# mLSTM cell and multiplicative FFN on one core: one lasting PSUM tile for the cell, outputs first on VectorE, and unread products on TensorE

## The chip, the cores and the metric

The kernel runs on one core of a Trainium2 chip. The metric is the device time of one execution in microseconds (us), the median of several runs. A core has five engines that work side by side: TensorE (PE in the profile; its weight loads are shown apart as PEld), VectorE (DVE), ScalarE (ACT), GpSimd (POOL) and SyncE (SP), which here only issues transfers (DMA). They meet through semaphores.

## The reference, cut to what matters

Attention block: a recurrent cell over 768 time steps, for 4 batches and 8 heads of 40 dimensions. Then a feed-forward block on the 3072 x 320 result.

```python
for t in range(S):
    m_new = np.maximum(f_gate[:, :, t] + m, i_gate[:, :, t])
    f_stab = np.exp(f_gate[:, :, t] + m - m_new)
    i_stab = np.exp(i_gate[:, :, t] - m_new)
    C = f_stab * C + i_stab * np.einsum('bhd,bhe->bhde', vt, kt)
    n = f_stab * n + i_stab * kt
    h_tilde = np.einsum('bhde,bhe->bhd', C, qt)
    denom = np.maximum(np.abs(np.einsum('bhd,bhd->bh', n, qt)), 1.0)
    y[:, :, t] = sigmoid(o_gate[:, :, t]) * h_tilde / denom
...
a = x @ w1; b = x @ w2
out = ((a * b) @ w3) @ w_out        # 320 -> 1024 -> 1024 -> 320
```

All inputs of the cell are 32-bit floats. The weights come as 64-bit floats and are turned into 32-bit ones on the chip.

## The kernel before

The recurrence is computed in chunks. A unit n is one batch and 128 time steps (two chunks of 64), all 8 heads; there are 24 units, n = 0 to 23, four batches after each other for each stretch of time. Within a unit everything is a matrix product:

- ss = k times q, 64 x 64 for each head and chunk; VectorE multiplies it into the weights `pw` (L348), which ScalarE made with exponentials and GpSimd cut to a triangle;
- pc = what the unit adds to the state, from `kbuf` and the weighted values `vw` (`weighted`, GpSimd, L302). VectorE adds its first half to the state (`second`, L352, or copies it for the first four units, L354), GpSimd decays that (`decayed`, L307), and VectorE adds the second half (`after`, L362);
- ph = `pw` times the values and pi = q times the states before: the two parts of the output, taken one step later. VectorE adds them into `h` (L369, L373), makes the divisor `den` (three small operations, L378 to L381), multiplies it with the output gate (`o_in`, L383) and writes `y` (L385).

All four share one tile `cell` of four PSUM banks: ss and pc lie in banks 0 and 1 (columns 0 to 255 and 256 to 419 of 512), pi and ph in banks 2 and 3. It comes from a pool with one buffer and is allocated anew in every step (L314), so a step's first cell product waits until the last reader of the step before is done.

The main loop runs over steps s = 0 to 29. Step s does, among other things: transfers for later units (SyncE); `turn` of unit s, eight transposes of k and q on TensorE (`pt`, L93) with copies on ScalarE (L297); transposes of finished outputs (`px`, `x_trans`); the feed-forward products `pa`, `pb` (`up`, `up_rest`), from step 4 on; then `quarter_work`, with ph and pi of unit s - 1 and pc and ss of unit s on TensorE, and VectorE's work on them; then pieces of the conversion of the weights (`convert`, four VectorE operations each, L187 to L190). Later steps add the products `wp` that fold w3 and w_out into one matrix, and `po`, the last product. Ahead of the loop stand the gates: scans and subtractions on VectorE and GpSimd (L496 to L511), and products that turn and spread their results (`pg`, `ub`, `pd`).

TensorE works through its products in the order in which they are written (`in_order`). The other engines take their instructions in the order that a scheduler chose while the kernel was built, and from step 17 on in the written order; `tc.issue_after(x)` puts what it encloses behind instruction x. The order of the work on the cell before, on TensorE: ph, pi, pc, ss. On VectorE: `pw` (L348), the pc addition or copy (L352, L354), the outputs (L369 to L385), and last the second pc addition (L362).

A 32-bit product with plain operands shows as two records of TensorE in the profile, a transpose as one.

Of the kernel before, what the change touches and what calls it, by code (L numbers as in the profile page):

```python
# [8 lines left out]
FP = mybir.dt.float32  # L9
U32 = mybir.dt.uint32  # L10
AF = mybir.ActivationFunctionType
OP = mybir.AluOpType
# [4 lines left out]
def kernel(  # L17
# [26 lines left out]
    nc = tc.nc  # L44

    B, H, S, D = q.shape
    L = 64
    P = 128
    NT = S // L
    NT2 = S // P  # L50
    NU = NT2 * B
    NP = H // 2
    DP = 64
    D1 = D + 1
    DM = H * D
# [4 lines left out]
    REM = DM - KF * P  # L60
# [7 lines left out]
    sb = ctx.enter_context(tc.tile_pool(name="sb", bufs=2))  # L68
# [3 lines left out]
    ps_c = cell_psum.enter_context(tc.tile_pool(name="ps_c", bufs=1, space=bass.MemoryType.PSUM))  # L72
    banks = [ps_m]

    def mps(shape, name):
        pool = banks.pop(0)
        banks.append(pool)
        return pool.tile(shape, FP, name=name, tag="m")
# [3 lines left out]
    def in_order(ins):  # L82

        if last:
            tc.add_manual_dep(ins.ins, last.pop().name, mybir.DependencyInfo(
                mybir.DependencyClass.NoSync, mybir.DependencyReason.DATA), reason="in_order")
        last.append(ins.ins)

    def mm(out, lhsT, rhs, start=True, stop=True):
        in_order(nc.tensor.matmul(out, lhsT=lhsT, rhs=rhs, start=start, stop=stop))  # L90

    def transpose(out, in_, n=P):
        in_order(nc.tensor.transpose(out, in_, ident[0:n, 0:n]))  # L93

    halves = [slice(0, L), slice(L, P)]
    heads = [slice(0, D), slice(DP, DP + D)]
    quarters = ((0, 0), (1, 1), (0, 1), (1, 0))
# [8 lines left out]
    ident = const.tile([P, P], FP, name="ident")  # L106
# [10 lines left out]
    o_t, u_t = {}, {}  # L117
# [60 lines left out]
    def to_f32(dst, raw):  # L178
# [6 lines left out]
        r = wst.tile([128, n], U32, name="ma", tag="ma", bufs=1)  # L185
        V = nc.vector
        V.tensor_scalar(out=t, in0=hi, scalar1=3, scalar2=None, op0=OP.logical_shift_left)  # L187
# [70 lines left out]
    qT_t, kT_t, vw_t, before_t, y_t, x_t = {}, {}, {}, {}, {}, {}  # L258
# [51 lines left out]
    def quarter_work(s, rest):  # L310


        rest()
        t = ps_c.tile([P, 4, 512], FP, name="cell", tag="cell")  # L314

        def part(j, c0, n):
            return t[:, j:j + 2, c0:c0 + NP * n].rearrange("p x (n d) -> p x n d", d=n)

        ss, pc, pi = part(0, 0, L), part(0, NP * L, D1), part(2, 0, D1)
        ph = [t[halves[x], 2 + x, NP * D1:(NP + H) * D1].rearrange("p (h d) -> p h d", d=D1) for x in range(2)]  # L320
        n = s - 1
        if 0 <= n < NU:
            pw, vt, qT = u_t.pop(n), vbuf[n % NB], qT_t.pop(n)
            before = before_t.pop(n)
            for hd in range(H):
                for x, r in enumerate(halves):
                    mm(ph[x][:, hd, :], pw[r, hd, :], vt[r, hd, :])
            for p in range(NP):
                for hip, x in quarters:
                    mm(pi[halves[x], hip, p, :], qT[heads[hip], p, halves[x]], before[x][heads[hip], p, :])  # L330
        n, first_read = s, None
        if n < NU:
            c, b = divmod(n, B)
            kt, vw = kbuf[n % NB], vw_t.pop(n)
            ends = range(2 if c < NT2 - 1 else 1)
            first, second, after = state[b]
            before_t[n] = first, second
            state[b] = after, second, first
            for p in range(NP):
                for x, e in quarters:  # L340
                    if x in ends:
                        mm(pc[halves[e], x, p, :], kt[halves[x], 2 * p + e, :], vw[halves[x], 2 * p + e, :])
            kT, qT, pw = kT_t.pop(n), qT_t[n], u_t[n]
            for p in range(NP):
                for hip, x in quarters:
                    mm(ss[halves[x], hip, p, :], kT[heads[hip], p, halves[x]], qT[heads[hip], p, halves[x]])
            pv = pw.rearrange("p (n two) t -> p two n t", two=2)
            first_read = nc.vector.tensor_tensor(out=pv, in0=ss, in1=pv, op=OP.mult)  # L348
            with tc.issue_after(first_read.ins):

                if c:
                    nc.vector.tensor_tensor(out=second, in0=pc[:, 0], in1=second, op=OP.add)  # L352
                else:
                    nc.vector.tensor_copy(out=second, in_=pc[:, 0])  # L354
                if len(ends) > 1:
                    decayed(after, second, n, 1)
        done = None
        with tc.issue_after(first_read.ins) if first_read else nullcontext():
            if 0 <= s - 1 < NU:
                done = outputs(s - 1, pi, ph)  # L360
            if n < NU and len(ends) > 1:
                done = nc.vector.tensor_tensor(out=after, in0=pc[:, 1], in1=after, op=OP.add)  # L362
        return done

    def outputs(n, pi, ph):
        c, b = divmod(n, B)
        hs = slice(b * H, (b + 1) * H)
        h = sb.tile([P, H, D1], FP, name="h", tag="h")
        nc.vector.tensor_tensor(out=h.rearrange("p (n two) d -> p two n d", two=2), in0=pi,  # L369
                                in1=gT[:, c, hs].rearrange("p (n two) -> p two n", two=2).unsqueeze(3)  # L370
                                .to_broadcast([P, 2, NP, D1]), op=OP.mult)
        for x, r in enumerate(halves):
            nc.vector.tensor_tensor(out=h[r], in0=ph[x], in1=h[r], op=OP.add)  # L373

        den = sb.tile([P, H, 1], FP, name="den", tag="den")
        nc.vector.tensor_scalar(out=den.bitcast(U32), in0=h[:, :, D:D1].bitcast(U32), scalar1=0x7FFFFFFF, scalar2=None,  # L378
                                op0=OP.bitwise_and)
        nc.vector.tensor_scalar(out=den, in0=den, scalar1=1.0, scalar2=2.0, op0=OP.max, op1=OP.mult)  # L380
        nc.vector.reciprocal(out=den, in_=den)  # L381
        e = o_t.pop(n)
        nc.vector.scalar_tensor_tensor(out=e, in0=e, scalar=1.0, in1=den.to_broadcast([P, H, D]), op0=OP.add, op1=OP.mult)  # L383
        y_t[n] = sb.tile([P, DM + REM], FP, name="y", tag="y")
        return nc.vector.tensor_tensor(out=y_t[n][:, 0:DM].rearrange("p (h d) -> p h d", d=D), in0=h[:, :, 0:D], in1=e,  # L385
                                op=OP.mult)

    def send(n):

# [89 lines left out]
    def traced():  # L479
        return nc.cur_bb.bb.instructions  # L480
# [10 lines left out]

    f3, F3, U3, a3, w3d = (x.rearrange("p (c t) -> p c t", t=L) for x in (f_sb, F, U, a, w))
    V = nc.vector
    front = len(traced()) - 1

    V.tensor_copy(out=f_sb[third[0], 0:1], in_=a[third[0], 0:1])  # L496
# [4 lines left out]
    for i, r in enumerate(third):  # L501
        V.tensor_tensor_scan(out=M[r, 1:GC + 1], data0=F3[r, :, L - 1], data1=U3[r, :, L - 1], initial=M[r, 0:1],
                             op0=OP.add, op1=OP.max)
# [25 lines left out]
    for i, r in enumerate(third):  # L529
        nc.gpsimd.tensor_tensor(out=pick[r, :, i, :], in0=pair[r].to_broadcast([BH, B * NP, GC]), op=OP.mult,  # L530
                        in1=dec[r].unsqueeze(1).to_broadcast([BH, B * NP, GC]))
# [167 lines left out]
```

## Time and profile before

| what | value |
|---|---|
| median of 5 runs | 472.37 us (470.68 to 474.1) |
| the profiled execution | 469.81 us |
| its span on the core | 467.8 us |
| TensorE busy | 444.8 us, 95% of the span |
| VectorE busy | 257.8 us, 55% |
| ScalarE, GpSimd busy | 134.4 us, 82.2 us |
| moved by DMA | 52.72 MB, mean 113 GB/s |
| chain that ended last | PE 93%, issue 2%, all others 1% or less each |

A span is the time from the first to the last instruction of the profiled execution; the time of the run includes a little that lies around it (here 2.0 us). Busy times count the engine's records, which for TensorE overlap with its weight loads. The chain that ended last goes back from the last instruction, at each step to what released it. The slices cut the span into 40 equal parts of 11.7 us. The clock row gives what the throttle granted TensorE, in tenths of its full speed.

### The profile page before, as it was taken

To read this page: it belongs to the slowest core of one execution; us is meant where nothing else is said; L and a number is where in the kernel's file an instruction comes from. 1 tells how busy PE (TensorE), PEld (TensorE's weight loads), DVE (VectorE), ACT (ScalarE), POOL (GpSimd) and SP (SyncE) were. 2 spreads that over 40 slices of the span, in tenths; PEclk is the share of its full clock that TensorE was granted. 3 is DMA by queue.
4 is the path that set the end of the run, shared out by engine and by line. 5 is a ranking of instruction groups with operands and counts; after the bars stand their busy time and mean duration, and the time that the engine had idled before them with its cause. 6 is when DMAs were issued, how large, how long until landed. Compare 5 with 4: busy or idle time off the path is not lost.

```text
span 467.8 us, 12799 instructions
## 1 busy us (share of the span) xinstructions
PE 444.8 (95%) x5319; PEld 357.2 (76%) x5319; DVE 257.8 (55%) x515; ACT 134.4 (29%) x376; POOL 82.2 (18%) x156
## 2 busy tenths in 40 slices
PE   2866999999999999999999999999999999999997
PEld 2765788888778788887878777787777877868864
DVE  7675589888988988898832451615426134011110
ACT  3743274444443144223451230211101101011111
POOL 5341222222220222022161110200000000000000
PEclk9995699999999999999999999999999999999999
DMA  9999958688978677686452535444121120200001
GB/s 189 174 175 221 177 88 159 143 186 176 206 185 197 147 167 157 160 161 137 102 114 67 129 81 133 91 107 105 33 63 32 32 63 1 62 15 14 1 14 44
DMA packets 136554, 52.72 MB, mean 113 GB/s; under 512 B 109936, under 2 KB 127536, under 8 KB 136496
## 3 DMA queue, kind: packets, MB, share of 16 engines
q1 hardware_dynamic: 132896, 47.87, 50.0%
q10 hardware_dynamic: 3600, 4.03, 2.5%
q8 instruction: 42, 0.69, 0.7%
q14 instruction: 16, 0.13, 0.1%
HBM read 46.07 MB, written 5.80 MB: 111 GB/s over the span
## 4 chain that ended last, share of the span: by engine, by line
PE 93%; issue 2%; DVE 1%; POOL 1%; DMA 1%; ACT 1%; SPq 0%; POOLq 0%; DVEq 0%; ACTq 0%
PE pa L90 27%; PE po L90 23%; PE pb L90 18%; PE cell L90 13%; PE wp L90 7%; PE pt L93 2%; PE px L93 1%; DMA kbuf<-in_k_dram 1%; PE ub L90 1%; POOL pw L280 1%; POOL vw L302 0%; ACT pw L278 0%; SPq L444 0%; ACT qT L297 0%; PE pg L93 0%
## 5 line engine op out<-in xcount | busy, mean ns | idle before, releaser
L569 DVE TENSOR_TENSOR ab<-pb,a_sb 128x512 f32<-128x512 f32 x48 | 32.7, 689 | 139.5 <-ACT a_sb L568 139.5
L90 PE MATMUL po<-w3o,ab 128*128 128x320 f32 x384 | 106.2, 435 | 0.0
L90 PEld LDWEIGHTS po<-w3o,ab 128*128 128x128 f32 x384 | 72.1, 190 | 30.1 <-ACT a_sb L568 0.4
L90 PE MATMUL pa<-xT,w 128*128 128x256 f32 x384 | 92.8, 385 | 0.6 <-ACT xT L423 0.6
L90 PE MATMUL pb<-xT,w 128*128 128x256 f32 x384 | 90.7, 379 | 0.0
L90 PEld LDWEIGHTS pa<-xT,w 128*128 128x128 f32 x384 | 73.4, 193 | 13.5 <-ACT xT L423 1.0
L90 PEld LDWEIGHTS pb<-xT,w 128*128 128x128 f32 x384 | 73.0, 190 | 10.1
L568 ACT ACTIVATE a_sb<-pa 128x512 f32<-128x512 f32 x48 | 28.7, 598 | 169.0 <-PE pb L90 169.0
L307 POOL TENSOR_TENSOR state<-state,decay 128x164 f32<-128x164 f32 x40 | 22.0, 549 | 202.2 <-DVE state L352 133.2
L90 PE MATMUL pa<-xT,wr 64*64 64x256 f32 x384 | 47.0, 383 | 0.0
L90 PE MATMUL pb<-xT,wr 64*64 64x256 f32 x384 | 47.0, 383 | 0.0
L278 ACT ACTIVATE pw<-pw,aT 128x64 f32<-128x64 f32 x160 | 40.3, 337 | 14.3 <-DMA pw<-U_d 14.3
L90 PEld LDWEIGHTS pa<-xT,wr 64*64 64x64 f32 x384 | 25.8, 132 | 16.8 <-issue 7.8
L90 PE MATMUL wp<-wo,w3T 128*128 128x320 f32 x128 | 35.9, 433 | 0.6 <-DVE ab L569 0.6
L280 POOL TENSOR_SCALAR_AFFINE_SELECT pw<-pw 64x512 f32<-64x512 f32 x48 | 33.1, 690 | 18.6 <-ACT pw L278 17.0
L90 PEld LDWEIGHTS cell<-vbuf,pw 64*64 64x64 f32 x768 | 27.2, 140 | 8.6 <-issue 5.7
L348 DVE TENSOR_TENSOR pw<-cell,pw 128x512 f32<-128x512 f32 x24 | 16.6, 691 | 30.6 <-PE cell L90 30.6
L576 ACT COPY o_sb<-po 128x320 f32<-128x320 f32 x24 | 10.1, 422 | 75.4 <-PE po L90 75.4
L90 PE MATMUL cell<-vbuf,pw 64*64 64x41 f32 x768 | 27.2, 230 | 4.7 <-issue 4.7
L90 PEld LDWEIGHTS wp<-wo,w3T 128*128 128x128 f32 x128 | 23.7, 190 | 9.7 <-DVE ab L569 0.9
L90 PEld LDWEIGHTS pb<-xT,wr 64*64 64x64 f32 x384 | 25.8, 132 | 0.0
L373 DVE TENSOR_TENSOR h<-cell,h 64x328 f32<-64x328 f32 x48 | 23.9, 497 | 1.1
(90 smaller groups left out, 456.3 us busy)
## 6 DMA issues: line engine op xcount, KB each, us to landing
raw<-in_moe_w_dram SPq DMA_DIRECT2D x64, 128.0 KB, 3.1
pw<-U_d SPq DMA_DIRECT2D x40, 128.0 KB, 4.1
kbuf<-in_k_dram SPq DMA_DIRECT2D x24, 160.0 KB, 4.5
vbuf<-in_v_dram SPq DMA_DIRECT2D x24, 160.0 KB, 5.1
o_in<-in_o_gate_dram SPq DMA_DIRECT2D x24, 160.0 KB, 4.5
out_dram<-o_sb ACTq DMA_DIRECT2D x24, 160.0 KB, 2.0
raw<-in_moe_w_dram SPq DMA_DIRECT2D x7, 512.0 KB, 5.7
raw<-in_moe_w_out_dram SPq DMA_DIRECT2D x32, 80.0 KB, 3.0
```

The source lines that it names most:

```text
L90: in_order(nc.tensor.matmul(out, lhsT=lhsT, rhs=rhs, start=start, stop=stop))
L93: in_order(nc.tensor.transpose(out, in_, ident[0:n, 0:n]))
L278: nc.scalar.activation(out=pw[:, h, :], in_=src[:, h, :], func=AF.Exp, bias=aT[:, c, b * H + h:b * H + h + 1])
L280: nc.gpsimd.affine_select(out=pw[r], in_=pw[r], compare_op=OP.is_ge, fill=0.0, base=0, pattern=[[0, H], [1, L]], channel_multiplier=-1)
L307: nc.gpsimd.tensor_tensor(out=new, in0=old, op=OP.mult, in1=decay[:, b * NP:(b + 1) * NP, 2 * c + x:2 * c + x + 1] .to_broadcast([P, NP, D1]))
L348: first_read = nc.vector.tensor_tensor(out=pv, in0=ss, in1=pv, op=OP.mult)
L373: nc.vector.tensor_tensor(out=h[r], in0=ph[x], in1=h[r], op=OP.add)
L568: nc.scalar.mul(out=a_sb, in_=pa, mul=UP ** -2)
L569: nc.vector.tensor_tensor(out=ab_t[gr][j][:, fs[0]:fs[-1] + 1, t0:t0 + a_sb.shape[-1]], in0=pb, in1=a_sb, op=OP.mult)
L576: nc.scalar.copy(out=o_sb, in_=po)
```

## The change

The tile `cell` is allocated once, ahead of all loops, and used in every step. `keep_warm(times)` adds products of the identity with 92 of its own columns into columns 420 to 511 of bank 0 of `cell`, which nobody reads: 14 ahead of the gates' first instruction, and 3 in each of the steps 0 to 3, ahead of the step's cell products. On TensorE, ss now comes before pc. `outputs` is cut into three parts: h (its three operations) at once, then `first` (the divisor), then `then` (`o_in` and `y`). On VectorE the new order of a step is h, `pw`, the first pc addition or copy, the divisor, the second pc addition, `o_in`, `y`.

```diff
+    cell = ps_c.tile([P, 4, 512], FP, name="cell", tag="cell")
...
+    def keep_warm(times):
+        for _ in range(times):
+            mm(cell[:, 0, NP * (L + D1):512], ident, ident[:, 0:512 - NP * (L + D1)])
...
         rest()
-        t = ps_c.tile([P, 4, 512], FP, name="cell", tag="cell")
+        if s < B:
+            keep_warm(3)
+        t = cell
...
+            kT, qT, pw = kT_t.pop(n), qT_t[n], u_t[n]
+            for p in range(NP):
+                for hip, x in quarters:
+                    mm(ss[halves[x], hip, p, :], kT[heads[hip], p, halves[x]], qT[heads[hip], p, halves[x]])
             for p in range(NP):
                 for x, e in quarters:
                     if x in ends:
                         mm(pc[halves[e], x, p, :], kt[halves[x], 2 * p + e, :], vw[halves[x], 2 * p + e, :])
-            kT, qT, pw = kT_t.pop(n), qT_t[n], u_t[n]
-            for p in range(NP):
-                for hip, x in quarters:
-                    mm(ss[halves[x], hip, p, :], kT[heads[hip], p, halves[x]], qT[heads[hip], p, halves[x]])
+        den = None
+        if 0 <= s - 1 < NU:
+            den = outputs(s - 1, pi, ph)
+        if n < NU:
             pv = pw.rearrange("p (n two) t -> p two n t", two=2)
             first_read = nc.vector.tensor_tensor(out=pv, in0=ss, in1=pv, op=OP.mult)
...
-        done = None
-        with tc.issue_after(first_read.ins) if first_read else nullcontext():
-            if 0 <= s - 1 < NU:
-                done = outputs(s - 1, pi, ph)
+            if den:
+                done = den()
             if n < NU and len(ends) > 1:
-                done = nc.vector.tensor_tensor(out=after, in0=pc[:, 1], in1=after, op=OP.add)
-        return done
+                nc.vector.tensor_tensor(out=after, in0=pc[:, 1], in1=after, op=OP.add)
+            if den:
+                done = done()
+        return done if den else first_read
...
+    keep_warm(14)
     front = len(traced()) - 1
```

In the built program, the cell's first product of a step (in steps 1 to 3 now the first unread one) waits for the step before's second pc addition, and h waits for the last product of its step. The two reductions that make `pair` and `odd` (L474, L476), which stood at the head of VectorE's order, now stand behind the gates' last subtraction (L511). In SyncE's order, some of the later transfers of k (`load_turned`, from the tenth unit on) stand behind the transfers of a step's output instead of ahead of them. Nothing else moves.

## The prediction

> **What bounds the kernel now.** I read the page's slices first, then the busy time by stretch, then the chain of waits and the timeline of the one place where TensorE is not full. The slices (11.7 us each):
>
> ```profile
> PE   2866999999999999999999999999999999999997
> DVE  7675589888988988898832451615426134011110
> PEclk9995699999999999999999999999999999999999
> DMA  9999958688978677686452535444121120200001
> ```
>
> TensorE is full from the sixth slice on, at full clock. Only the first five hold anything to win, and two of those show a granted clock near half. Closer (us, then busy time and count for TensorE, its weight loads, VectorE, ScalarE, GpSimd; clock; DMA share; GB/s):
>
> ```profile
> 25.00:30.00 5.00, 3.73 (x120) 3.05 (x112) 2.95 (x7) 1.67 (x9) 1.55 (x3) 1.00 0.94 182
> 30.00:35.00 5.00, 2.35 (x111) 2.39 (x115) 4.70 (x10) 2.16 (x6) 2.67 (x4) 0.94 1.05 172
> 40.00:45.00 5.00, 3.04 (x86) 3.07 (x89) 3.84 (x10) 3.26 (x11) 0.24 (x1) 0.50 1.27 190
> 50.00:55.00 5.00, 4.43 (x13) 3.31 (x12) 4.68 (x12) 1.06 (x2) 2.57 (x5) 0.52 0.92 175
> 55.00:60.00 5.00, 5.00 (x145) 4.31 (x146) 1.13 (x2) 2.36 (x8) 0.00 (x0) 1.00 1.31 171
> 60.00:120.00 60.00, 58.91 (x1010) 50.48 (x1002) 53.74 (x118) 30.68 (x86) 16.89 (x30) 1.00 0.73 154
> ```
>
> From 60 us to the end TensorE is busy 403.5 of 407 us, so a step that arrives there earlier ends the kernel earlier by as much. Between 30 and 55 us it both waits and runs at half clock. What half clock costs, in the chain of waits (start, us, what):
>
> ```profile
> 48.14 1.91 PE pt L93 x8
> 51.24 3.75 PE pa L90 x8
> 69.27 1.02 PE pt L93 x8
> 70.29 1.73 PE pa L90 x8
> ```
>
> And why it waits, in the timeline around step 1 (start, us, engine, line, operation, idle before it):
>
> ```profile
> 27.55 0.69 DVE L348 TENSOR_TENSOR pw<-cell,pw 128x512 f32<-128x512 f32 x1 [1.97 <-PE cell L90]
> 28.40 0.49 DVE L369 TENSOR_TENSOR h<-cell,gT 128x328 f32<-128x328 f32 x1
> 30.61 0.72 DVE L383 SCALAR_TENSOR_TENSOR o_in<-o_in,den 128x320 f32<-128x320 f32 x1
> 31.36 0.82 DVE L385 TENSOR_TENSOR y<-h,o_in 128x320 f32<-128x320 f32 x1
> 32.22 0.33 DVE L362 TENSOR_TENSOR state<-cell,state 128x164 f32<-128x164 f32 x1
> 32.61 1.00 PEld L90 LDWEIGHTS cell<-vbuf,pw 64*64 64x64 f32 x31 [2.89 <-issue]
> ```
>
> TensorE ended step 1's cell products at 27.39; the next cell product starts when VectorE's last read of the cell banks (L362) ends at 32.55. The profile calls this "issue", but it is VectorE's chain of 5.2 us. After step 2 the same chain runs 37.36 to 41.86, 4.5 us, and is behind the gap up to 41.96.
>
> **What the Trainium skill says.** "TensorE: Matmul & The Clock Gate", Part 1: TensorE runs at half rate until it has been busy for a window of some 3.4 us, falls back after an idle window, and the windows run free of the kernel. The trace agrees on the factor two (above) and roughly on the length: the rates drop near 34.3 after 2.7 us of idleness and recover near 54.7, 3.5 us into products without a hole. It also shows a limit: 3.5 us of small products (ub, 17.8 to 21.4) stayed slow, so busy in the records is not surely busy for the gate. Before 24 us the clock column says 1.00, yet 32 ub products take 1.91 us at 8.78 and 1.08 us at 27.39: it was cold. The same page, Part 4, says transposes do not count as busy in the same way; no stretch here holds transposes alone. "PSUM — Partial Sum Buffer", PSUM bank collisions: engines must be kept apart by bank and quadrant, not by address. So unread products in an unused corner of bank 0 wait for bank 0's readers; in the built program they wait for the last reader of the whole tile.
>
> **The change part by part.** *VectorE's order.* The outputs' first three operations (h) now come first, e and y last; the pc1 addition, which frees the banks, stands before e and y. The built program makes h wait for the step's very last product, so nothing starts sooner; the banks are free sooner by e, y and gaps: 0.72 + 0.82 + 0.06 = 1.6 us after step 1, 0.49 + 0.49 + 0.07 = 1.05 after step 2. GpSimd's decay (0.46 us after pc0) is covered by three small operations, 0.17 + 0.17 + 0.20 us; if that fails, it costs 0.2. The chain is then some 3.5 us. y comes 0.3 us later relative to the banks; only step 5 has a px close behind it (a wait of 0.45 at 65.3), so 0.3 us there, elsewhere nothing: the other px take older tiles. pw comes 1.5 us later, read a step later.
>
> *ss before pc on TensorE.* pc waited for vw at 15.36 (1.55 us) and 26.23 (0.98). ss needs only qT, so up to 1 us of it moves into these waits.
>
> *One lasting tile.* No instruction; the waits between steps stay.
>
> *The pair and odd reductions* move behind the gate chain on VectorE (0.25 + 0.24 us at 8.42). pick started at 8.74 and still can; VectorE has 3.5 us free before 17.51. Nothing.
>
> *The unread products.* One f32 product is two records (weights 128 columns, 92 columns moving). No row has this shape. By the pt rows (128 columns of weights) a record is 1.91 / 8 = 0.24 us cold and 0.127 warm. Moving time alone, from pa, would be 92/256 of 0.47 = 0.17 cold, so weights bind; bounds 0.17 and 0.28, I take 0.24 and 0.12. Fourteen in front are 28 records, 6.7 us cold, from 1.6 us (identity ready at 1.54) to 8.3 at the latest, less if the clock rises meanwhile. The gates' first product came at 8.20: cost 0 to 0.2 us, cover TensorE's empty start. Three in each of steps 0 to 3 cost 1.4 us cold or 0.7 warm; as they wait for the banks they fill no bank wait, and in steps 2 and 3 stand on the path. In steps 0 and 1 they lie largely beside waits for qT and vw.
>
> **The sum.** Cold, the triple (1.4) eats what VectorE's order gives (1.6 and 1.05). The change pays by the clock. With the front products TensorE has no hole from 1.6 to 13.8 us, so I expect it warm at 7 to 12. Then ub(0) ends 0.8 earlier; the exps can start when ScalarE is free (10.07 instead of 10.80), and vw and pc follow by 0.7; step 0's cell ends near 15.8, not 17.34. In step 1 ScalarE's 16 exps, a scaling that needs a weight piece, and v(1) hold it: warm TensorE then idles about 2 us before qT and can lose the clock. Step 1 ends near 25.3 (2.1 early). Step 2: banks at 28.8; ub, pt and the triple leave no hole, so the clock is likely back while the cell products run: about 0.9 + 3.3 + the 1.2 us pause that stood inside this group at 35.58 (no wait in the profile, DMA full): 34.2, that is 3.2 early. Step 3: banks 3.5 later (37.7), triple and products 3.4 warm to 5.5 cold, 4.5 taken (a 2 us hole lies ahead), again a 1.2 us pause (46.06 before): 43.4, 4.7 early. Step 4 took 12.3 us from there to 60.45, of which the 3.75 pa would be 1.73 if warm; half of that and the pt gain: 11.6, ending at 55.0: 5.4 us early. From there TensorE is full. Profiled execution: span 467.8, with what lies around it 469.81; minus 5.4 is 464.4. That execution lies 2.6 us under the median of 472.37; against the median, **467.0**.
>
> **The rivals.** *The clock holds throughout.* Triple and products warm, 3.4 instead of 4.5 us in step 3 (42.3), step 4 in 9.7, with pt, px and pa at the rates of step 5: it ends at 52.0, 8.4 early: 464.0 against the median. For: the triples are there, and rates held at 65% busy windows (27.5 to 30.9). Against: a 2 us hole before each bank release, since the triple waits too.
>
> *Loads take the place.* DMA is over 0.9 busy in nearly every stretch to 60 us. k(3) was issued at 29.18 and takes 4.5 us, used at 37.3; k(6) at 54.38, used at 69.2. Those leave 3.6 and 10 us, so an advance beyond about 4 us can be clipped in steps 3 to 6; v(3), issued until 32.7, gates vw(3). Clipped to 1.5 us: 470.9.
>
> *Slower: triples on the path at half clock.* Place: steps 1 to 3, ahead of the first ph product. Price 1.4 each, 4.2, against 1.6 + 1.05 + 0.4; and if warm idling ahead of qT drops the clock at 24 instead of 34, step 2's ub, pt and ph run cold, 2.6 more: 3.8 later, less 1 us from ss: 475.2. It decides if less than one window in steps 2 and 3 is full.
>
> **How the numbers follow.** Forecast 0.47 (own range 464.5 to 469.8), clock held 0.24, loads 0.19, slower 0.10. About 0.5%, 2.4 us, is what a measurement of this kernel can tell from no change (its five runs spread over 3.4 us). Faster: 0.45 + 0.24 + 0.04 = 0.73; same 0.02 + 0.15 + 0.01 = 0.18; slower 0.09. The range, 461.8 to 471.6, takes in most of the held clock and of the loads; what is left out is mainly the slower case and the best of the held clock.
>
> **What would show it.** ub(0) in 1.1 us rather than 1.9 (front works); bank release 3.5 us after each cell group; clock column at 1.00 in part of 30 to 55; pa in step 4 at 1.7 or 3.75; step 4's cell end at 55. Wrong if TensorE's clock falls before 30 us and stays, if TensorE waits for kbuf or vbuf in steps 3 to 6, or if the total from step 5 to the end, 407 us, changes: then my claim that all lies in the first 60 us fails.

## The result and the profile after

| | before | after |
|---|---|---|
| median of the comparison | 470.72 us (79 runs) | 468.21 us (44 runs) |
| lowest, highest | 465.71, 474.76 us | 465.88, 470.92 us |
| ratio of the times | | 0.9963, 95% interval 0.9949 to 0.9976 |
| profiled execution, its span | 469.81, 467.8 us | 467.89, 466.1 us |

The change makes the kernel faster, by 2.5 us by the medians. Runs that lie over 1.5% above a kernel's fastest are left out of every ratio, and as the kernel before spreads over 9 us this leaves out more of its runs than of the others', so that a ratio shows less of a gain than the medians do (here 1.7 us). The kernel before was timed again with each group of experiments (its medians are 470.1 to 471.5 us). Below I give how far each kernel's median lies under that one, with the ratio and its interval behind it; differences under about 1 us between groups are not read.

The slices of the changed kernel, 11.65 us each:

```profile
PE   8697989999999999999999999999999999999997
DVE  6757898989988988898823350614416134011110
PEclk9977999999999999999999999999999999999999
DMA  8989997788995677597452625544021120200001
```

TensorE is at work from the first slice (the unread products in front), and two slices show the clock column at 7 in place of one at 5 and one at 6. The busy times by stretch of the changed kernel, with the columns as in the prediction:

```profile
25.00:30.00 5.00, 5.00 (x144) 4.92 (x142) 1.24 (x3) 0.84 (x2) 0.34 (x1) 0.50 0.85 163
30.00:35.00 5.00, 4.19 (x123) 3.79 (x124) 4.83 (x11) 3.65 (x12) 3.00 (x5) 0.98 0.94 183
40.00:45.00 5.00, 4.95 (x118) 4.78 (x120) 3.22 (x6) 1.15 (x2) 0.60 (x2) 0.54 0.93 132
50.00:55.00 5.00, 5.00 (x104) 4.23 (x107) 4.13 (x6) 1.72 (x6) 2.17 (x4) 1.00 0.91 133
60.00:120.00 60.00, 56.28 (x967) 47.86 (x966) 54.26 (x111) 28.28 (x79) 16.57 (x28) 1.00 0.81 167
```

Two places differ from the plan. From 25 to 30 us, where the kernel before ran at full clock, TensorE is busy without a hole but at half clock. And from 60 to 120 us it is busy 56.28 us, not 58.91: a loss in the part that I had called full. The transposes and the first feed-forward products of steps 4 and 5, in the chain of waits of the changed kernel:

```profile
45.76 1.78 PE pt L100 x8
48.63 1.99 PE pa L92 x8
...
66.36 1.02 PE pt L100 x8
67.38 1.73 PE pa L92 x8
```

pa of step 4 took 1.99 us, not 3.75: there the clock is up. The timeline around step 1's end, changed kernel:

```profile
28.72 0.50 DVE L383 TENSOR_TENSOR h<-cell,gT 128x328 f32<-128x328 f32 x1 [4.71 <-PE cell L92]
30.29 0.69 DVE L361 TENSOR_TENSOR pw<-cell,pw 128x512 f32<-128x512 f32 x1
31.94 0.28 DVE L374 TENSOR_TENSOR state<-cell,state 128x164 f32<-128x164 f32 x1
32.27 0.91 PE L92 MATMUL cell<-ident 128*128 128x92 f32 x6 [0.81 <-DVE state L374]
32.65 0.82 DVE L405 TENSOR_TENSOR y<-h,o_in 128x320 f32<-128x320 f32 x1
```

The cell products ended at 28.64 and the banks were free at 32.22: 3.6 us, where the old order took 5.2. The unread triple stands first behind the release. Step by step (end of the step's cell products, us):

| | step 0 | 1 | 2 | 3 | 4 | from there to the end |
|---|---|---|---|---|---|---|
| before | 17.35 | 27.39 | 37.36 | 48.14 | 60.39 | 407.4 |
| forecast | 15.8 | 25.3 | 34.2 | 43.4 | 55.0 | 407 |
| after | 16.28 | 28.64 | 35.64 | 45.76 | 56.01 | 410.1 |

So this execution was 4.4 us ahead when step 4 ended, against 5.4 in the forecast, and then lost 2.7 us. On the way, step 1 ended 1.25 us later than before. TensorE's waits in the changed kernel up to 64 us (us in total, times, longest) name two of the places:

```profile
PE cell L92 <- DVE state L374: 3.8, 2, 3.0
PE pt L100 <- DMA kbuf<-in_k_dram: 3.3, 1, 3.3
PE px L100 <- POOL y L435: 1.1, 1, 1.1
...
PE px L100 <- DVE y L405: 0.6, 1, 0.6
```

The prediction did not count k of unit 1 among the waits, and px waited 0.45 us before.

### The profile page after: what moved, and what is told of

It reads as the page before. It is cut to its first block, busy times and chain, and to the rows that moved or that the text cites. A ratio compares the mean times of both kernels' runs of the same rounds, so it can differ in the third digit from the quotient of the medians.

```text
span 466.1 us, 12891 instructions
## 1 busy us (share of the span) xinstructions
PE 448.5 (96%) x5371; PEld 362.5 (78%) x5371; DVE 262.2 (56%) x515; ACT 134.3 (29%) x376; POOL 82.6 (18%) x156
## 4 chain that ended last, share of the span: by engine, by line
PE 88%; DMA 4%; SPq 3%; DVE 2%; ACT 1%; issue 1%; POOL 1%; ACTq 0%
PE pa L92 27%; PE po L92 23%; PE pb L92 18%; PE cell L92 11%; PE wp L92 7%; DMA w3o<-in_moe_w_dram 2%; SPq L133 2%; PE pt L100 1%; PE px L100 1%; DMA kbuf<-in_k_dram 1%; DMA pw<-U_d 1%; SPq L178 1%; SPq L153 0%; ACT pw L285 0%; DVE ma L195 0%
## 5 line engine op out<-in xcount | busy, mean ns | idle before, releaser
L92 PE MATMUL pa<-xT,w 128*128 128x256 f32 x384 | 91.0, 380 | 0.8 <-ACT xT L445 0.8
L92 PEld LDWEIGHTS pa<-xT,w 128*128 128x128 f32 x384 | 72.3, 190 | 13.1 <-ACT xT L445 1.0
L314 POOL TENSOR_TENSOR state<-state,decay 128x164 f32<-128x164 f32 x40 | 19.2, 481 | 211.3 <-DVE den L395 159.2
L287 POOL TENSOR_SCALAR_AFFINE_SELECT pw<-pw 64x512 f32<-64x512 f32 x48 | 35.3, 735 | 13.3 <-ACT pw L285 11.8
L383 DVE TENSOR_TENSOR h<-cell,gT 128x328 f32<-128x328 f32 x24 | 12.0, 498 | 25.1 <-PE cell L92 25.1
```

The lines of the kernel that those rows point to most:

```text
L287: nc.gpsimd.affine_select(out=pw[r], in_=pw[r], compare_op=OP.is_ge, fill=0.0, base=0, pattern=[[0, H], [1, L]], channel_multiplier=-1)
L314: nc.gpsimd.tensor_tensor(out=new, in0=old, op=OP.mult, in1=decay[:, b * NP:(b + 1) * NP, 2 * c + x:2 * c + x + 1] .to_broadcast([P, NP, D1]))
```

## The experiments

Each edit is shown against the kernel that the text names.

**Orders or unread products.** Four kernels take the change apart; all are shown against the changed kernel. The first leaves out all unread products and keeps the two new orders and the lasting tile:

```diff
-        if s < B:
-            keep_warm(3)
...
-    keep_warm(14)
```

> The change without any unread product: new orders and the lasting tile alone. If the orders make the gain (banks released 1.6 and 1.05 us sooner after steps 1 and 2, ss ahead of pc), it is 1.5 to 3 us faster than before, ratio 0.994 to 0.997. If the clock makes it, the clock drops in step 1 or 2 and stays low until the first pa, as before, and the later px in step 5 (62.56 in the changed kernel) takes back what the banks gave: ratio 0.998 to 1.002.

Measured: 465.24 us, 6.0 less than before (ratio 0.9864, 0.9828 to 0.9901). It beats the changed kernel by 3 us.

The second keeps the unread products and the tile, with both old orders:

```diff
-            kT, qT, pw = kT_t.pop(n), qT_t[n], u_t[n]
-            for p in range(NP):
-                for hip, x in quarters:
-                    mm(ss[halves[x], hip, p, :], kT[heads[hip], p, halves[x]], qT[heads[hip], p, halves[x]])
             for p in range(NP):
                 for x, e in quarters:
                     if x in ends:
                         mm(pc[halves[e], x, p, :], kt[halves[x], 2 * p + e, :], vw[halves[x], 2 * p + e, :])
...
+            kT, qT, pw = kT_t.pop(n), qT_t[n], u_t[n]
+            for p in range(NP):
+                for hip, x in quarters:
+                    mm(ss[halves[x], hip, p, :], kT[heads[hip], p, halves[x]], qT[heads[hip], p, halves[x]])
...
+            if 0 <= s - 1 < NU:
+                done = outputs(s - 1, pi, ph)
             if n < NU and len(ends) > 1:
-                nc.vector.tensor_tensor(out=after, in0=pc[:, 1], in1=after, op=OP.add)
+                done = nc.vector.tensor_tensor(out=after, in0=pc[:, 1], in1=after, op=OP.add)
```

> The kernel before with the lasting tile and all unread products (14 in front, 3 in each of steps 0 to 3), orders on TensorE and VectorE as before. If the clock makes the gain: 2 to 4 us faster, ratio 0.991 to 0.996, as px in step 5 is not delayed. If the orders make it: the triples stand on the path, 0.7 to 1.4 us in each of steps 2 and 3, ratio 0.999 to 1.005.

Measured: 470.78 us, 0.5 less than before (0.9976, 0.9952 to 1.0000).

The third keeps only the 14 front products, the fourth only the triples, both with the new orders and the tile:

```diff
-        if s < B:
-            keep_warm(3)
```

> The changed kernel without the triples; the 14 products in front stay. If only the front lifts the clock (up at 13 us), step 0 is 1 us earlier but the wait for k of unit 1 (3.3 us before 21.9) drops it again, so this equals the version without unread products within 0.5 us. If the triples matter, the clock is not back at 30 and the time is 1 to 3 us above the changed kernel, ratio to before 0.998 to 1.003.

```diff
-    keep_warm(14)
```

> The changed kernel without the 14 products in front. If the front is worthless or harmful (it makes TensorE reach the wait for k of unit 1 early and lose the clock there), this is as fast as the changed kernel or up to 1.5 us faster: ratio to before 0.992 to 0.997, and the clock is high from about 24 us through step 1. If the front is what pays, 1 to 2 us slower than the changed kernel: 0.998 to 1.002.

Measured: front alone 465.47 us (5.8 less than before; 0.9866, 0.983 to 0.9902); triples alone 470.09 us (1.2 less; 1.0044, 1.0009 to 1.0079).

What follows: the front products neither win nor lose by themselves. The triples cost 5 us without them and 3 us with them. That the unread products pay is refuted: without any of them the kernel is faster.

**Which order.** Old VectorE order, ss ahead of pc on TensorE, lasting tile, no unread products. Shown is what differs from the kernel before with the lasting tile:

```diff
-            for p in range(NP):
-                for x, e in quarters:
-                    if x in ends:
-                        mm(pc[halves[e], x, p, :], kt[halves[x], 2 * p + e, :], vw[halves[x], 2 * p + e, :])
             kT, qT, pw = kT_t.pop(n), qT_t[n], u_t[n]
             for p in range(NP):
                 for hip, x in quarters:
                     mm(ss[halves[x], hip, p, :], kT[heads[hip], p, halves[x]], qT[heads[hip], p, halves[x]])
+            for p in range(NP):
+                for x, e in quarters:
+                    if x in ends:
+                        mm(pc[halves[e], x, p, :], kt[halves[x], 2 * p + e, :], vw[halves[x], 2 * p + e, :])
```

> The kernel before with the lasting tile and one more edit: on TensorE ss ahead of pc; VectorE's order as before, no unread products. Theory A (VectorE's order carries the gain of about 6 us that the two orders show together): the vw waits of steps 0 and 1 shrink by up to 1 us each, but the bank release stays 5.2 us after step 1's cell end, so the time is within 1.5 us of the kernel before (470.0 to 471.3). Theory B (ss first carries it: TensorE has no hole in front of pc, and VectorE's pw can start earlier): 466 to 467, and the cell ends of steps 1 and 2 come 1 us or more earlier than 27.39 and 37.36.

And VectorE's new order alone, same tile; against the kernel without unread products, it is the same move the other way round:

```diff
-            for p in range(NP):
-                for hip, x in quarters:
-                    mm(ss[halves[x], hip, p, :], kT[heads[hip], p, halves[x]], qT[heads[hip], p, halves[x]])
             for p in range(NP):
                 for x, e in quarters:
                     if x in ends:
                         mm(pc[halves[e], x, p, :], kt[halves[x], 2 * p + e, :], vw[halves[x], 2 * p + e, :])
+            for p in range(NP):
+                for hip, x in quarters:
+                    mm(ss[halves[x], hip, p, :], kT[heads[hip], p, halves[x]], qT[heads[hip], p, halves[x]])
```

> The kernel before with the lasting tile and VectorE's new order alone; TensorE keeps pc ahead of ss, no unread products. Theory A (VectorE's order carries the gain): bank release some 3.5 us after each cell end, time 465 to 467, within 1.5 us of the kernel with both orders (465.24). Theory B (ss first carries it): 469 to 470.5. Either way px of step 5 is late, by two waits of some 0.6 and 1.1 us, since GpSimd's decay follows the first pc addition.

Measured: 465.49 us (5.6 less; 0.9913, 0.9889 to 0.9936) and 466.08 us (5.0 less; 0.9901, 0.988 to 0.9923). Each alone brings nearly all that both bring together. Neither theory had that, and it pointed at what both kernels share: the tile.

Two more start from the kernel without unread products: GpSimd's copy of y at the head of the step, and six unread products in each of steps 2 and 3 that go to a rotating bank and so wait for nothing of the cell:

```diff
+        if 0 <= s - 2 < NY:
+            twice(s - 2)
...
-        elif 0 <= s - 2 < NY:
-            twice(s - 2)
```

> Both new orders and the lasting tile, no unread products, and one edit more: GpSimd's copy of y is issued at the head of its step, ahead of the weighting of v and the decay. Theory (VectorE's new order delays GpSimd's queue, and so step 5's px, by 1.6 us): the wait of 1.07 us on GpSimd ahead of px's later transposes goes, step 5's cell ends 1 us earlier than 64.33, and the time falls by about 1 us, from 465.24 to 464.2. Rival (TensorE meets another wait right behind, or loads take the place): 465 to 466.

```diff
+        warm = mps([P, 512 - NP * (L + D1)], "warm")
         for _ in range(times):
-            mm(cell[:, 0, NP * (L + D1):512], ident, ident[:, 0:512 - NP * (L + D1)])
+            mm(warm, ident, ident[:, 0:512 - NP * (L + D1)])
...
+        if 2 <= s < B:
+            keep_warm(6)
```

> Both new orders and the lasting tile, and 6 unread products in steps 2 and 3, written to a tile of the rotating four-bank pool, so that they wait for no bank of the cell and lie in the waits for the release (1.52 and 0.93 us without unread products). Theory path (unread products cost what stands behind the release): they cost at most 0.5 us in each step, time 464.5 to 466.5, against 468.21 of the changed kernel. Theory clock (filled waits keep the clock up): no drop of the granted clock between 30 and 50 us, 1 to 3 us faster than 465.24. Rival (any unread product costs, by its number): 12 products are 24 records of 0.12 us or more, 3 us or more slower than 465.24.

Measured: 465.47 us (5.6 less) and 467.67 us (3.4 less). The copy's wait of 1.07 us at px went, and the median did not follow. The filled waits cost 2.6 us: from step 1's end to the next cell product they added 0.55 us (4.17 against 3.62), after step 2 nothing (4.48 against 4.54). That is less than the loss. The profile shows part of the rest: this kernel is 1.1 us ahead of the one without unread products when step 4 ends (53.06 against 54.12), and then TensorE stops at 63.15 for 0.94 us inside step 5's products, without a wait. What such stops are is told next.

**The tile alone.** The kernel before, with the tile allocated once and nothing else:

```diff
+    cell = ps_c.tile([P, 4, 512], FP, name="cell", tag="cell")
...
-        t = ps_c.tile([P, 4, 512], FP, name="cell", tag="cell")
+        t = cell
```

> The kernel before with the lasting tile alone: both old orders, no unread products. It is the control for the kernels with one new order each, which both gained 5 us. Theory (the tile itself is worth nothing; each order alone already takes nearly all that there is to gain): within 1 us of the kernel before, 470 to 472. Rival (the gain that both orders share is the tile's, and the unread products took it back where old orders and unread products stood together): 465 to 467.

Measured: 466.81 us, 3.9 less than before (0.9935, 0.9912 to 0.9959). Its 22 runs lie between 463.39 and 468.55 us, the 63 of the kernel before between 465.54 and 475.13. The edit that I had put at nothing carries the larger part of the gain. The rival that the scheduler gave the other engines another order falls: in the two traces the instructions of VectorE, ScalarE, GpSimd and SyncE (518, 406, 165 and 424, without those for semaphores) stand in the same order. The built programs show how they differ: a tile allocated anew makes the first cell product of steps 2 and 3 wait for three semaphores (a transfer, VectorE, TensorE's own earlier work), the lasting tile for two. The Trainium skill ("Perfetto Trace Analysis", Identifying Dependency Chains) says that an instruction waiting on several engines may get semaphore instructions of their own in front of it. So it is in these traces: before, the instruction in front takes the transfer and VectorE, and TensorE's own semaphore stays on the product; with the tile kept, it takes the transfer alone and is over in 0.05 us, and VectorE's stays on the product. The chain of waits shows the two cases. First the kernel before (start, us, what):

```profile
29.98 2.66 issue
32.65 2.93 PE cell L90 x118
35.58 1.29 issue
...
41.96 4.10 PE cell L90 x108
46.06 1.17 issue
47.24 0.90 PE cell L90 x20
```

and the same stretch with the tile kept:

```profile
32.42 0.34 DVE state L364
32.76 0.04 issue
32.81 4.59 PE cell L92 x124
...
41.53 0.34 DVE state L364
41.87 0.04 issue
41.91 3.69 PE cell L92 x126
```

Before, the chain breaks off at "issue": the wait sits in a semaphore instruction of TensorE's sequencer (the trace has one of 3.46 us from 29.13 and one of 4.86 us from 37.05), which the chain cannot pass. With the tile kept no such record of more than 0.15 us stands between 12 and 62 us, and the chain goes on through VectorE. And 2.9 and 4.1 us after the release, TensorE stops inside a group of products for 1.29 and 1.17 us with no wait at all; with the tile kept it doesn't.

What it lacks there is instructions. One queue of instructions, TensorE's by its count, moved 0.69 MB in 42 packets, 16 KB each, one for 253 of the 10,638 product and weight records; the same skill ("Advanced Engine Details and Errata", ISA Cache) gives 16 KB, 256 instructions, as the line that is fetched. The stops lie at the ends of such lines: if all of TensorE's records are counted from the start (products, weights, semaphores), the kernel before resumes after its two stops at records 962 and 1218, 256 apart. The changed kernel resumes at 3265 after a stop of 0.96 us (103.25), and the kernel with filled waits at 1985 after the one at 63.15: multiples of 256 further on, but for one record. And each of the four resumes 1.3 to 1.6 us after the end of a fetch. The DMA view of the kernel with the tile kept, from 30 to 32.9 us, has one such fetch (the trace puts it at 31.22), so it lies within the wait:

```profile
q8 instruction: 1, 0.02, 2.5%
```

In the kernel before it comes at 34.38, 1.7 us behind the release (the view from 33 to 34.6 us), and the products that it brings are late:

```profile
q8 instruction: 1, 0.02, 4.1%
```

The Trainium skill ("Perfetto Trace Analysis", Per-engine timelines) gives a reason: an instruction of the sequencer alone holds it until its wait is over, while a product is put into a wait queue, which frees the sequencer for the next. The fetch times agree with that; the wait queue itself no run here shows. The page has the profiler leave the wait of such an instruction out of its record; in these traces the record holds it (3.46 and 4.86 us).

**Is it that semaphore?** Three kernels. Both new orders, no unread products, the tile anew in each step, against the kernel without unread products:

```diff
-        t = cell
+        t = ps_c.tile([P, 4, 512], FP, name="cell", tag="cell")
```

> Both new orders, no unread products, and the tile allocated anew in every step as before. In the built program the first cell product of steps 2 and 3 then waits for three semaphores (a transfer, VectorE, TensorE itself) instead of two, and TensorE gets a semaphore instruction of its own ahead of it. Theory semaphore (that instruction holds back the instructions behind it, and their fetch comes late, so that a pause of 1.2 us follows inside the products of steps 2 and 3; the lasting tile is worth 4 us by that): 468 to 470, against 465.24 with the lasting tile, with pauses labelled issue between 30 and 50 us. Rival (the tile helps the old orders only, the floor of 465 holds): 465 to 466.5.

The kernel before with one tile for steps 0 to 3, a new one in each later step, and the reverse (in the second the condition is `s <= B`):

```diff
+        if s == 0 or s >= B:
+            kept[:] = [ps_c.tile([P, 4, 512], FP, name="cell", tag="cell")]
-        t = ps_c.tile([P, 4, 512], FP, name="cell", tag="cell")
+        t = kept[0]
```

> The kernel before with one tile for the steps 0 to 3 and a new one in every step from 4 on: the third semaphore goes in steps 2 and 3, and stays in the late steps. Theory semaphore (steps 2 and 3 carry it all): 466 to 467.5, as with the tile lasting throughout (466.81). Rival (the gain lies in the late steps, where TensorE is full): 470 to 471.5.

> The kernel before with a new tile in each of the steps 0 to 4 and the last of them kept to the end: the third semaphore stays in steps 2 and 3 and goes in the late steps. Theory semaphore: 470 to 471.5, as before, with pauses of 1.2 us inside the products of steps 2 and 3. Rival (late steps): 466 to 467.5.

Measured: 469.93 us (1.5 less than before; 0.9995, 0.9966 to 1.0024), 466.49 us (5.0 less; 0.9921, 0.9893 to 0.995) and 471.97 us (0.5 more; 1.0042, 1.0012 to 1.0072). All three fall on the side of the semaphore theory, the last 0.5 us above its range: the tile is worth 4 to 5 us under the old orders and under the new, and all of it that can be told comes from steps 2 and 3. In the traces the long semaphore waits stand in the first and the third (2.56 and 3.76 us; 3.51 and 4.85 us) and are gone in the second. The chain of waits of the first of them, new orders and new tiles, has the stops again:

```profile
33.56 0.56 PE cell L90 x24
34.12 2.43 issue
36.55 0.45 PE cell L90 x8
...
44.70 0.94 issue
45.64 0.87 PE cell L90 x21
```

How the 4 to 5 us divide is not settled. In the profiles of the kernel before and of the tile kept alone, the second is 2.5 us ahead when step 3 ends (45.59 against 48.14), which is as long as the two stops together, and step 4 adds 2.3 us (10.0 against 12.3), with the clock up again at 46.38 instead of 54.83. In the profile with the late steps kept, the stops are only 0.45 and 0.35 us, and the clock is at half until 54.34 us. That the stops cause the low clock is not shown: without unread products the clock was down for 17 us (31.72 to 48.78) with no stop at all, and with the early steps kept step 4 took 12.4 us, again without one.

**A better order.** On VectorE pw and the first pc addition ahead of h, then h, the divisor, the second pc addition, `o_in`, `y`; ss first, lasting tile, no unread products. Against the kernel without unread products:

```diff
-        if 0 <= s - 1 < NU:
-            den = outputs(s - 1, pi, ph)
...
-            if den:
+            if 0 <= s - 1 < NU:
+                den = outputs(s - 1, pi, ph)
                 done = den()
```

> Lasting tile, ss ahead of pc, no unread products, and a third order on VectorE: pw and the first pc addition ahead of h as before, then h, the divisor, the second pc addition, and e and y last. It frees the banks as early as the changed order, and lets GpSimd's decay start 1.5 us earlier. Theory (the changed order gives back 1.6 us in step 5 by delaying GpSimd): the wait on GpSimd at step 5's px goes, time 463.5 to 464.5, 1 us or more under the 465.24 of both new orders. Rival (all these orders end at the same floor of about 465, set by the loads): 464.8 to 466.

Measured: 465.03 us, 5.7 less than before (0.9904, 0.987 to 0.9938). Its lowest and highest runs are 463.75 and 465.84. By the medians no kernel here is faster, but it cannot be told from the one without unread products: the floor of the rival.

**What the triples cost, and where.** The changed kernel with triples in steps 0 and 1 only, and with six products instead of three:

```diff
-        if s < B:
+        if s < 2:
             keep_warm(3)
```

> The changed kernel with the unread triples in steps 0 and 1 only. Theory (the triples cost where they stand behind the bank release, in steps 2 and 3, 0.9 and 1.3 us): 465.5 to 466.5, against 468.2 of the changed kernel and 465.5 of the one with the front products alone. Rival (the price is in steps 0 and 1, where they delay the first units, or is spread): 467 to 468.5.

```diff
-            keep_warm(3)
+            keep_warm(6)
```

> The changed kernel with six unread products instead of three in each of the steps 0 to 3. Theory (each triple costs its own duration behind the bank release, 0.9 to 1.3 us a step, in three of four steps): 471 to 472, some 3 us above the changed kernel's 468.2. Theory clock (more unread products fill more windows): fewer us at half clock, and 468 or less. Rival (the price of the first triple is the wait that it takes on, not its length): 468 to 469.5.

and later the other half, triples in steps 2 and 3 only:

```diff
-        if s < B:
+        if 2 <= s < B:
             keep_warm(3)
```

> The changed kernel with the triples in steps 2 and 3 only; it answers to the one with triples in steps 0 and 1 only (467.33) and the one with none (465.47, front products alone). If the prices add up: 466.0 to 466.6, as the changed kernel is at 468.2. If the triples of steps 2 and 3, behind the bank release, carried the price, as the forecast's rival had it: 467.5 to 468.5. If one pair of triples costs as much as all: 467 to 467.6.

Measured: 467.33 us (3.4 less than before; 0.9946, 0.9923 to 0.9969), 467.61 us (3.1 less; 0.9961, 0.9932 to 0.999), 466.88 us (3.2 less; 0.9951, 0.9927 to 0.9976). With the front alone it was 5.8 less: so one pair of triples costs about 2.5 us, the other as much, and both 3.3. They don't add up, and twice the length costs no more. In the six-product profile the clock stays up from 33.36 us to the end, so that a clock that holds may pay the added length back; but its 22 runs spread from 464.84 to 472.89 us, and one profile does not show it for the others. Late instruction fetches may be another part of the price: stops at the ends of fetched lines stand in seven of the nine profiles with unread products in steps 0 to 3 and the tile kept (0.75 to 2.18 us in sum), and in three of the eight with the tile kept in steps 0 to 3 and no such products (0.18 to 1.10). No run tests that by itself.

Step 1 shows how a triple gets on the path. TensorE's rows of the changed kernel:

```profile
21.92 0.66 PE L100 MATMUL pt<-ident,kbuf 128*128 128x128 f32 x4 [3.31 <-DMA kbuf<-in_k_dram]
22.59 0.63 PE L100 MATMUL pt<-ident,q_all 128*128 128x128 f32 x4
23.06 1.15 PE L92 MATMUL cell<-ident 128*128 128x92 f32 x6
24.14 1.83 PE L92 MATMUL cell<-vbuf,pw 64*64 64x41 f32 x30
```

and of the kernel without unread products:

```profile
20.52 1.10 PE L100 MATMUL pt<-ident,kbuf 128*128 128x128 f32 x4
21.43 0.63 PE L100 MATMUL pt<-ident,q_all 128*128 128x128 f32 x4
21.99 1.07 PE L92 MATMUL cell<-vbuf,pw 64*64 64x41 f32 x30
```

Behind the transposes nothing waits: the triple pushes ph by 1.08 us. And the clock, which had been up, fell at 23.36, after the wait of 3.31 us for k of unit 1, so that the step's products ran at half rate. Of the kernels with ss first and k loaded as before, the five with a triple in step 1 end its cell products at 28.64 to 29.88 us, the eight without at 26.03 to 28.82.

**Is k of unit 1 the stop?** The changed kernel with that unit's transfers ahead of two weight pieces:

```diff
+    load(1)
     fetch("w12", 3, 0)
     fetch("w12", 4, 0)
-    load(1)
```

> The changed kernel with the transfers of unit 1 (k, q, v) issued ahead of two weight pieces. Theory loads (whatever TensorE gains in step 0 ends at k of unit 1, which lands at 20.5 to 22 us in every kernel, so front products and triples cannot pay): step 1's transposes start near 19, TensorE's wait of 3.3 us at 18.6 us goes, and the time falls by 1 to 2 us, to 466 to 467. Rival (qT, vw or ScalarE's 16 exponentials hold step 1 just as long, or the weight pieces are now late): 468 to 470.

Measured: 468.84 us (2.6 less than before; 0.9981, 0.995 to 1.0012), no better than the changed kernel. TensorE's wait in this kernel has only moved:

```profile
PE cell L92 <- ACT qT L304: 3.4, 1, 3.4
```

ScalarE waits 2.53 us for a weight piece, then makes 16 exponentials (3.37 us) and only then copies qT; step 1 ends at 27.52 us instead of 28.64. So k is what step 1 waits for first, and ScalarE is next: most of what TensorE gains in step 0, by front products or otherwise, ends there. In this profile the clock was also at half from 23.28 to 54.00 us, more than twice as long as in the changed kernel, so its total does not say what the earlier k is worth alone.

**The late y.** The changed kernel, unread products and all, with pw and the first pc addition ahead of h:

> The changed kernel with all its unread products, and with pw and the first pc addition ahead of h on VectorE, so that step 5's px does not wait 1.66 us (0.59 and 1.07). Theory tail (in the profiles of two kernels with triples, the clock fell to half near 64 us, after those two waits, which costs 3.4 us more; so the price of the unread products is largely paid there): 465 to 466, close to the 465.03 without unread products. Theory path (the triples cost where they stand, up to step 3): 467 to 468.5.

Measured: 466.19 us, 3.9 less than before (0.9921, 0.9888 to 0.9953), against 2.5 for the changed kernel. The timeline of the changed kernel around step 5's px shows what is queued on GpSimd:

```profile
58.67 0.46 POOL L314 TENSOR_TENSOR state<-state,decay 128x164 f32<-128x164 f32 x1 [6.41 <-DVE den L395]
59.08 1.51 POOL L287 TENSOR_SCALAR_AFFINE_SELECT pw<-pw 64x512 f32<-64x512 f32 x2
60.68 0.85 POOL L309 TENSOR_TENSOR vw<-vbuf,wT 128x328 f32<-128x328 f32 x1
61.08 0.41 PE L100 MATMUL px<-ident,y 128*128 128x128 f32 x2 [0.59 <-DVE y L405]
61.49 0.64 POOL L314 TENSOR_TENSOR state<-state,decay 128x164 f32<-128x164 f32 x1
62.07 0.43 POOL L435 COPY y<-y 128x64 f32<-128x64 f32 x1
62.56 0.33 PE L100 MATMUL px<-ident,y 128*128 128x128 f32 x1 [1.07 <-POOL y L435]
```

and with pw first:

```profile
61.30 0.30 POOL L434 COPY y<-y 128x64 f32<-128x64 f32 x1 [0.48 <-DVE y L404]
61.42 0.56 PE L100 MATMUL px<-ident,y 128*128 128x128 f32 x3
```

The decay waits for the first pc addition, which now stands behind h and pw; behind the decay stand the selects, vw, another decay, and then the copy of y's last columns that px needs. With pw first, px does not wait. The unread products then cost 1.8 us instead of 3.5. Without unread products the same reorder, and the earlier copy, won nothing in the median, so the full price of the late y is seen only beside them; why is open. The trace offers one lead: in two profiles with triples (triples alone, and triples in steps 0 and 1) the clock fell to half for 6.8 us from 64.94 and 63.55, just behind the px waits; in the profile of the changed kernel it did not.

## Why the prediction was wrong, and what in it held

The forecast gain was 5.4 us, from 472.37 to 467.0; against the median of the comparison, 470.72, it would have ended at 465.3. Measured were 2.5 us. Two steps of the sum failed, in opposite directions. By the prediction's own prices the orders were worth some 3 us (1.6 + 1.05 for VectorE's, 0.4 for ss) and the tile nothing, which leaves, as an estimate, 2.4 us for the unread products and the clock. Measured, as differences between the gains above, were 2.1, 3.9 and -3.5 us, which make up the 2.5. (Step 4 of the kernel before ends at 60.39 us in its rows, not at the 60.45 of the sum; nothing rests on it.)

- **"The change pays by the clock": this step failed, and is the largest miss.** Without unread products the gain is 6.0 us, with them 2.5: they cost 3.5 us where the sum had counted on them. The clock did not rise at 7 to 12 us: ub(0) at 8.73 still took 1.98 us, where 1.1 was to show that the front works, and by the rates it rose at about 13.1. It fell at 23.36, rose at 30.19 and was down again from 40.43 to 47.26; pa in step 4 took 1.99 us, as hoped. But a higher clock did not make the kernel faster. The one without unread products was at half clock longer (31.72 to 48.78) and had ended step 3 at 41.70 us, 4.1 earlier than the changed one; 1.4 of that is k of unit 1, which came sooner in that execution (20.52 against 21.92). Step 4's warm products won back 2.2.
- **"One lasting tile. No instruction; the waits between steps stay": this step failed too.** Put at 0, it measured 3.9 us alone, and 4.5 as the difference under the new orders (6.0 against 1.5). The waits stay, but VectorE's moves from a semaphore instruction onto the product itself. With that went the two pauses of some 1.2 us that I had seen, found no wait for, and carried over into steps 2 and 3 of the sum; and the word "issue" in front of step 2's cell products, which I had explained away, was the trace of that semaphore instruction.
- **VectorE's order: right in its mechanism.** The chain was to be 3.5 us; it measured 3.6 after step 1. After step 2 it was 4.4, since VectorE was in a weight conversion until 36.6 when the products ended at 35.64. Both orders on top of the tile brought 2.1 us (6.0 less 3.9).
- **The triples' own size: right** (0.7 warm to 1.4 cold foreseen, 0.83 to 1.28 measured), and the front's (6.7 foreseen, 6.28 measured). Their place was half wrong: in step 1 they did not lie beside a wait.
- **Step 0 and 1: wrong.** Front products were to end step 0 at 15.8; it ended at 16.28, and at 16.46 without them: ss first does it. Step 1 was to gain 2.1 us and lost 1.25, since its transposes waited for k. I had looked for a load as a rival, but in steps 3 to 6.
- **"y comes 0.3 us later ... so 0.3 us there": too small.** Two waits of 0.59 and 1.07 us in place of one of 0.45. I counted VectorE's place of y and not GpSimd's queue behind the first pc addition.
- **From 60 us on nothing changes: not so.** 410.1 instead of 407.4 us: 1.2 for px, 0.96 for a stop without a wait inside step 8's products at 103.25, 0.45 more ahead of wp at 117.5.

That the measured time lies only 1.2 us from the forecast 467.0 is luck: a gain of some 4 us that was not in the sum met a cost of some 3.5 us that stood in it as a gain, and the kernel before measured 1.65 us lower than it had in the five runs that I knew. Of the rivals, "triples on the path" described what the triples do, and "loads take the place" what step 1 does.

## What to carry to other kernels

Where the profile says "issue" in front of a product that must be waiting for something, count its semaphores: where the long wait had an instruction of its own, the next fetch of instructions came late here, and a tile kept through the loop instead of a new one in each step took that away. Products that nobody reads must pay for their length and for the transfers that they only reach sooner; try the kernel without them before believing in the clock. When an operation moves on one engine, follow the queue of the engine that it releases, down to the last user.

## What was unexpected

- Whole pauses of 0.2 to 2.4 us inside a group of products, without a wait, from instruction fetches of 16 KB that come late: they fall at places 256 records apart, but which of these places has one differs between kernels (35.58 and 46.06 before, 103.25 after, 34.12 with new tiles under the new orders). A semaphore in front is not the only cause: the kernel with pw first and no unread products, the fastest by its median, has one of 1.10 us at 34.41 without it.
- The granted clock doesn't rank these kernels. In the profiles, pw first without unread products had the lowest mean of four at 0.971 and the shortest span, 463.3 us; the changed kernel had 0.985 and 466.1, six unread products 0.989 and 465.5, the filled waits 0.989 and 464.9.
- The orders add little to the tile: tile 3.9 us, tile and ss first 5.6, tile and VectorE's order 5.0, all three 6.0. Whether the two orders add up lies within the 1 us that is not read.
